# Two output stores moved to ScalarE's queue, transposing loads re-placed among stores, and three PSUM copies moved from VectorE to ScalarE

## The chip, the cores and the metric

One core of a Trainium2 chip runs the kernel. The metric is the device time of one execution in microseconds. The engines are named as in the profile: PE (TensorE), DVE (VectorE), ACT (ScalarE), POOL (GpSimd) and SP (SyncE, which here only issues DMAs). "SPq" and "ACTq" are instructions that these two spend on issuing DMAs.

## What is computed

The reference is a forward pass and its gradients. Shortened to what matters here:

```python
xn = layernorm(x)                                   # x: 2048 x 512
k_shift = sum over t of k[s + t - 3] * shift_k[:, 3 - t]
kv = k_shift * v
y = irfft(rfft(kv) * rfft(ssm_k)) + kv * ssm_D      # a convolution of length 2048
out = x + xn * y + ((xn @ w_gate) * (xn @ w_up)) @ w_down   # F = 1376
grads = vjp(out)(grad_out)    # for x, k, v, shift_k, ssm_k, ssm_D, w_gate, w_up, w_down
```

The outputs that the change touches are out_7 and out_8 (gradients of w_gate and w_up, 512 x 1376), out_9 (gradient of w_down, 1376 x 512), out_4 (gradient of shift_k, 512 x 4) and out_6 (gradient of ssm_D, 512). Out_0 to out_3 and out_5 (the result and the gradients of x, k, v and ssm_k) are only moved against them in SP's queue.

## The kernel before, in words

The kernel has two stages. In the first, up to about 304 us, it normalises x, runs the gated layer forward and back in eight chunks of 256 rows (`ffn1`, `yb`), and takes the convolution's signals through a two-step transform by matmuls, with DRAM in between (FD, GD). The hidden rows and their gradients (`hd`, three tensors of 1376 rows) go to DRAM as HDD.

The last stage is what the change is about. It interleaves four streams of work, all in one program order that the loop at the end of the kernel writes out:

- `dw()` goes over the eleven blocks of 128 hidden rows (`FBLK`, the last has 96). For each block it needs the hidden rows turned, so that the sequence lies on the partitions. For blocks 0 to 6 PE turns them (`hid_t`: load hb, 16 transposes, copy by ACT to nath or natd). For the last four (`TURNED`, blocks 7 to 10) a transposing DMA loads them as natT (`load_t`), except for the last chunk, which PE turns (`last_t`, copied by ACT to nat7). Then `down_grad` sums 16 matmuls into pd, which ACT copies to od, stored to out_9, and four times 16 matmuls go into pu, which ACT copies to og. Two blocks share one og, which two DMAs store to out_7 and out_8.
- `inv_y` and `inv_dk` (lines 944 and 989) take the inverse transforms: pq is copied by ACT to yC or dd, po to o5t. `put_dD` turns a column of o5t by PE (ptd), copies it to dDt and stores it to out_6.
- `dsk_gram` makes the gradient of shift_k: for four blocks of 128 columns, 32 matmuls into pk; DVE multiplies the result by the identity, reading PSUM, into kd, and sums it up (dsk). At the end dsk is turned by PE (pts), copied to dskt and stored to out_4.
- `ew` runs `final` and `bwd` for eight row blocks: DVE work with a load bb each and three stores (o, e, dk). What they have to store is kept in `late` and put out at the start of the next turn by `put_late`.

The tile framework orders instructions by priority and dependencies and sets every wait. A block under `tc.high_priority` goes ahead of its place in the program. `tc.issue_after(x)` puts the instructions traced in it behind x, if they are on x's engine. A tile's buffer is given out again when all that read or wrote its last tenant is done, a store of it included. Tiles with the same `tag` share their buffers: `tag="dd"` has two, used in turn by dd, kd, nat7, dskt and the last og. PSUM has three double banks (`P2`) and two single ones (`P1`). Each DMA also waits, on one of eight semaphores used in turn, until the DMA that had this semaphore before has landed. The queues of SP and ACT are worked off in order.

Before the change SP issues all of these loads and stores but two, and the transposing loads are placed by `behind` (line 800): block 9 after the newest bb load, block 10 after the newest og store, blocks 7 and 8 where priority puts them.

Of the kernel before, what the change touches and what calls it, by code (L numbers as in the profile page):

```python
# [9 lines left out]
F32 = mybir.dt.float32  # L10
I32 = mybir.dt.int32
ALU = mybir.AluOpType
ACTF = mybir.ActivationFunctionType
AX = mybir.AxisListType
# [7 lines left out]
P = 128  # L22
NC4 = 4
FBLK = [(i * 128, min(128, F - i * 128)) for i in range((F + 127) // 128)]
NFB = len(FBLK)
NCH = 8
SOON = 300
# [163 lines left out]
def kernel(  # L191
# [24 lines left out]
    nc = tc.nc  # L216
# [17 lines left out]
    def act(o, i):  # L234
        nc.scalar.copy(o, i)  # L235

    def dve(o, i):
        nc.vector.tensor_copy(o, i)  # L238
# [4 lines left out]
    BX = dram.tile([P, R, 2, D], BF, name="BX")  # L243
# [11 lines left out]
    def P1(name, shape, dt=F32):  # L255
        return ps1.tile(shape, dt, name=name, tag="p1")

    ident = const.tile([P, P], BF, name="ident")
# [397 lines left out]
    first = ExitStack()  # L656
# [131 lines left out]
    LG = {}  # L788
# [9 lines left out]
    TURNED = range(NFB - 4, NFB)  # L798

    def behind(fb):  # L800
        first = {NFB - 2: lambda: LG["bb"], NFB - 1: lambda: LG["og"]}.get(fb)
        return tc.issue_after(first().ins) if first else ExitStack()

    def load_t(fb):

        f0, fw = FBLK[fb]
        if fb == SPLIT:
            parts = ((0, 5, "n", dict(tag="natd", bufs=2)), (5, NCH - 1, "n", dict(tag="nath")))
        elif fw < P:
            parts = ((0, NCH - 1, "n", dict(tag="natd", bufs=2)),)  # L810
        else:
            parts = ((0, NCH - 1, "b", dict(tag="hb")),)
        nats[fb, 0] = {}
        for a, e, pool, kw in parts:
            t = CP[pool].tile([P, e - a, 3, 2, fw], BF, name="natT", **kw)
            with behind(fb) as _, tc.high_priority(offset=SOON):
                nc.sync.dma_start_transpose(out=t[:].rearrange("s c t h f -> s (c t h) f"),
                                            in_=HDD[:fw, fb, a:e].rearrange("p c t s -> p (c t s)"))
            for c in range(a, e):
                nats[fb, 0][c] = t[:, c - a]  # L820
# [13 lines left out]
    def nat_h(fb, r):  # L834
        f0, fw = FBLK[fb]
        if fb not in TURNED:
            return nats[fb, 0][:, r, :fw]
        return nats[fb, 0][r // 2][:, 0, r % 2, :] if r < R - 2 else nats[fb, 1][:, 0, r % 2, :fw]
# [7 lines left out]
    def hid_t(fb, t):  # L846
        if fb in TURNED:
            return
        f0, fw = FBLK[fb]
        hb = hbs.pop(fb) if t == 2 else hbs[fb]  # L850
        if t == 0:
            nats[fb, 0] = CP["n"].tile([P, R, P], BF, name="nath")
        elif t == 1:
            nats[fb, 1] = CP["n"].tile([P, 2, R, P], BF, name="natd", bufs=2)
        dst = nats[fb, 0] if t == 0 else nats[fb, 1][:, t - 1]
        pt = P2("pt", [P, R, P], BF)
        for r in range(R):
            hs = hb[:fw, r // 2, t] if r < R - 2 else hds[1][:fw, fb, t]
            nc.tensor.transpose(pt[:, r, :fw], hs[:, (r % 2) * 128:(r % 2) * 128 + 128], ident[:fw, :fw])  # L859
        act(dst[:, :, :fw], pt[:, :, :fw])  # L860
# [56 lines left out]
    c2b = ctx.enter_context(tc.tile_pool(name="c2b", bufs=2, side="right", reuse_waits="tile"))  # L917
# [8 lines left out]
    dsk = c2.tile([P, NC4, 4], F32, name="dsk")  # L926
# [86 lines left out]
    def put_dD(o5t):  # L1013
        act(dDs[:], o5t[:, :, 0, 0])
        yield
        pt = P1("ptd", [P, P], BF)
        nc.tensor.transpose(pt[:NC4, :], dDs[:], ident[:])
        dDt = c2.tile([NC4, P], BF, name="dDt")
        dve(dDt[:], pt[:NC4, :])
        nc.sync.dma_start(out_6.rearrange("(c p) -> c p", p=128), dDt[:])  # L1020

    def down_grad(fb):
        f0, fw = FBLK[fb]
        pd = P1("pd", [P, D])
        for r in range(R):
            nc.tensor.matmul(pd[:fw, :], lhsT=nat_h(fb, r), rhs=goC[:, r, :], start=(r == 0), stop=(r == R - 1))  # L1026
            if r == R // 2 - 1 and fb:
                hid_t(fb, 2)
                if fb + 2 < NFB:
                    load_h(fb + 2)  # L1030
        od = c2b.tile([P, D], BF, name="od")
        if fb + 1 < NFB:
            act(od[:fw], pd[:fw])
            nc.sync.dma_start(out_9[f0:f0 + fw, :], od[:fw])
        else:
            for h, cp, q in ((0, act, nc.scalar), (1, dve, nc.sync)):
                hc = slice(256 * h, 256 * h + 256)
                cp(od[:fw, hc], pd[:fw, hc])
                q.dma_start(out_9[f0:f0 + fw, hc], od[:fw, hc])

    def load_h(fb):
        (load_t if fb in TURNED else load_hb)(fb)

    def dw():
        og = None
        load_hb(2)
        for fb, (f0, fw) in enumerate(FBLK):
            last = fb + 1 == NFB
            if not last:
                down_grad(fb)  # L1050
                yield
                hid_t(fb + 1, 0)
                hid_t(fb + 1, 1)
                yield
                yield
            pu = P2("pu", [P, NC4, 2, P])
            if fb % 2 == 0:
                og = c2b.tile([P, 2, NC4, P], BF, name="og1", tag="dd") if last else c2.tile([P, 2, NC4, 2 * P], BF, name="og")
            q0 = (fb % 2) * P
            for c in range(NC4):  # L1060
                for r in range(R):
                    nc.tensor.matmul(pu[:, c, :, :fw], lhsT=xnC[:, r, cs(c)], rhs=nat_d(fb, r),  # L1062
                                     start=(r == 0), stop=(r == R - 1))
                if c == 1:
                    yield
                    if fb + 1 in TURNED:
                        last_t(fb + 1)
                    yield
            act(og[:, :, :, q0:q0 + fw].rearrange("p t c f -> p c t f"), pu[:, :, :, :fw])
            if fb % 2 == 1 or last:  # L1070
                a = f0 - q0
                for t, o in enumerate((out_7, out_8)):
                    LG["og"] = nc.sync.dma_start(o[:, a:f0 + fw].rearrange("(c p) f -> p c f", p=128), og[:, t, :, :q0 + fw])
            yield
            if last:
                down_grad(fb)
                yield

    def dsk_gram():
        for c in range(NC4):  # L1080
            pk = P2("pk", [P, 2, D])
            for r in range(R):
                for h in range(2):
                    c0 = c * 128 + 64 * h
                    nc.tensor.matmul(pk[64 * h:64 * h + 64, h, 0:256], lhsT=dks[:, r, c0:c0 + 64],
                                     rhs=KH[0][:, r:r + 4, c0:c0 + 64], start=(r == 0), stop=(r == R - 1))
            kd = c2b.tile([P, 4, 64], F32, name="kd", tag="dd")
            with tc.high_priority(offset=SOON):
                for h in range(2):
                    hs = slice(64 * h, 64 * h + 64)  # L1090
                    nc.vector.tensor_tensor(kd[hs], pk[hs, h, 0:256].rearrange("q (j c) -> q j c", j=4),
                                            ident[hs, hs].unsqueeze(1).to_broadcast((64, 4, 64)), op=ALU.mult)
                nc.vector.tensor_reduce(dsk[:, c, :], kd[:], axis=AX.X, op=ALU.add)
            yield
        dskb = c2.tile([P, 4, NC4], BF, name="dskb")
        nc.vector.tensor_copy(dskb[:], dsk[:].rearrange("q c i -> q i c"))
        for _ in range(2):
            yield
        pt = P1("pts", [P, 4, P], BF)
        for j in range(4):  # L1100
            nc.tensor.transpose(pt[:NC4, j, :], dskb[:, 3 - j, :], ident[:])
        dskt = c2b.tile([NC4, P, 4], BF, name="dskt", tag="dd")
        dve(dskt[:], pt[:NC4].rearrange("c j q -> c q j"))
        nc.sync.dma_start(out_4.rearrange("(c p) j -> c p j", p=128), dskt[:])
        yield

# [17 lines left out]

    def load_fin(b):
        bb = c2b.tile([P, 2, 2, D], BF, name="bb")
        LG["bb"] = nc.sync.dma_start(bb[:], BX[:, 2 * b:2 * b + 2, :, :])
        FL[b] = bb

    def final(b):  # L1130
# [47 lines left out]
    def put_late():  # L1178
        for dst, t in late:
            nc.sync.dma_start(dst, t[:])  # L1180
        late.clear()

    def ew():
        with tc.issue_after(DKS[2].ins):
            load_fin(0)
        yield
        for f in tail:
            put_late()
            f()
            yield  # L1190
        with tc.issue_after(LG["og"].ins):
            put_late()
        yield
# [45 lines left out]
```

## Time and profile before

| | |
|---|---|
| median of 3 runs | 480.83 us (479.9 to 481.28) |
| profiled execution | 481.82 us |
| its span, first to last instruction | 480.03 us |
| granted TensorE clock | 0.999 |
| PE busy in 304 to 384, 384 to 432, 432 to 476 us | 79.32 of 80, 46.46 of 48, 43.63 of 44 us |
| ACT busy in the same stretches | 50.20, 18.08, 13.70 us |
| DVE busy in the same stretches | 32.79, 41.92, 37.27 us |
| DMA, mean over the span | 291 GB/s, 139.85 MB |

How to read it: the busy time of an engine says little on its own. A stretch is set by the engine that hardly waits in it; what it still waits for is in the view of waits, which gives for each waiting instruction the one that released it, the total, the count and the longest. In the timelines a row merges instructions of one kind: start, duration, engine, line, operation, output and inputs, count, and in brackets the idle time before it with its releaser. The duration of a merged row of matmuls runs to the end of the last one; the next starts a little sooner, since matmuls are pipelined. Some matmul records are missing, so that a run of eight can show seven.

### The profile page before, as it was taken

To read this page: it belongs to the slowest core of one execution; us is meant where nothing else is said; L and a number is where in the kernel's file an instruction comes from. 1 tells how busy PE (TensorE), PEld (TensorE's weight loads), DVE (VectorE), ACT (ScalarE), POOL (GpSimd) and SP (SyncE) were. 2 spreads that over 40 slices of the span, in tenths; PEclk is the share of its full clock that TensorE was granted. 3 is DMA by queue.
4 is the path that set the end of the run, shared out by engine and by line. 5 is a ranking of instruction groups with operands and counts; after the bars stand their busy time and mean duration, and the time that the engine had idled before them with its cause. 6 is when DMAs were issued, how large, how long until landed. Compare 5 with 4: busy or idle time off the path is not lost.

```text
span 480.0 us, 10366 instructions
## 1 busy us (share of the span) xinstructions
PE 464.5 (97%) x4252; PEld 311.6 (65%) x4293; DVE 340.5 (71%) x609; ACT 305.6 (64%) x349; POOL 14.0 (3%) x30
## 2 busy tenths in 40 slices
PE   7999999999999999999999999999999999999996
PEld 6867755547648447447447743576777687677885
DVE  7889989979366567686777877022257899599893
ACT  4957677659568678779779975375576535233141
POOL 8000000000000000000000000110000000000000
PEclk9999999999999999999999999999999999999999
DMA  8999999989998968968978379999899979999858
GB/s 268 374 381 366 310 296 320 315 300 328 318 288 270 277 202 255 285 200 245 298 235 259 118 272 331 388 329 313 312 361 364 371 260 320 318 267 239 252 155 294
DMA packets 111132, 139.85 MB, mean 291 GB/s; under 512 B 38859, under 2 KB 84336, under 8 KB 109550
## 3 DMA queue, kind: packets, MB, share of 16 engines
q1 hardware_dynamic: 109502, 137.85, 89.7%
q10 hardware_dynamic: 1584, 1.36, 1.0%
q8 instruction: 33, 0.54, 0.5%
q14 instruction: 13, 0.11, 0.1%
HBM read 67.08 MB, written 63.41 MB: 272 GB/s over the span
## 4 chain that ended last, share of the span: by engine, by line
PE 67%; DMA 15%; DVE 14%; issue 2%; SPq 2%; ACT 1%; DVEq 0%; ACTq 0%
PE px L555 15%; PE pgu L512 13%; PE pu L1062 8%; PE py L548 7%; PE pdh L518 6%; PE pd L1026 4%; PE ps L584 3%; DMA khC<-in_A_k_dram 3%; PE pg L613 3%; DMA ssk<-in_A_ssm_k_dram 2%; PE pf L370 2%; PE pt L859 2%; DMA vb<-in_A_v_dram 2%; DMA kb<-KS 2%; DMA x_b<-in_A_q_dram 2%
## 5 line engine op out<-in xcount | busy, mean ns | idle before, releaser
L555 PE MATMUL px<-WT,hd 128*128 128x512 bf16 (+1 forms) x340 | 78.6, 379 | 1.6 <-issue 1.4
L1062 PEld LDWEIGHTS <-xnC 128*128 128x128 bf16 x704 | 67.0, 98 | 8.4 <-issue 0.6
L555 PEld LDWEIGHTS <-hd 128*128 128x128 bf16 (+1 forms) x352 | 32.8, 98 | 44.4 <-issue 7.7
L235 ACT CAST gu<-pgu 128x1024 bf16<-128x1024 f32 (+1 forms) x48 | 45.4, 946 | 16.9 <-PE pgu L512 16.7
L235 ACT CAST GO<-pg 128x1024 bf16<-128x1024 f32 x48 | 46.2, 1015 | 13.8 <-issue 7.2
L235 ACT CAST SP<-ps 128x1024 bf16<-128x1024 f32 x47 | 45.5, 1025 | 13.7 <-PE ps L584 11.8
L512 PE MATMUL pgu<-xt,Wu 128*128 128x256 bf16 (+1 forms) x352 | 53.1, 273 | 1.1 <-DVE kn L238 0.6
L600 DVE TENSOR_TENSOR T<-SP 128x2048 bf16<-128x2048 bf16 x24 | 29.3, 1222 | 34.8 <-ACT SP L235 34.7
L512 PE MATMUL pgu<-xt,Wg 128*128 128x256 bf16 (+1 forms) x352 | 52.8, 273 | 0.0
L1062 PE MATMUL pu<-natd,xnC 128*128 128x256 bf16 x448 | 51.2, 273 | 0.0
L518 PE MATMUL pdh<-gt,WdT 128*128 128x256 bf16 (+1 forms) x352 | 46.9, 273 | 0.1
L235 ACT CAST fst<-pf 128x1024 bf16<-128x1024 f32 x44 | 42.7, 1031 | 5.5 <-issue 2.3
L512 PEld LDWEIGHTS <-Wu 128*128 128x128 bf16 (+1 forms) x352 | 33.0, 100 | 15.6 <-issue 10.7
L548 PE MATMUL py<-Wd,hd 128*128 128x512 bf16 (+1 forms) x167 | 40.2, 379 | 0.8 <-issue 0.5
L235 ACT CAST og<-pu 128x1024 bf16<-128x1024 f32 (+1 forms) x11 | 10.9, 993 | 43.7 <-PE pu L1062 28.3
L518 PEld LDWEIGHTS <-WdT 128*128 128x128 bf16 (+1 forms) x352 | 34.9, 100 | 4.8
L512 PEld LDWEIGHTS <-Wg 128*128 128x128 bf16 (+1 forms) x352 | 34.8, 100 | 3.7
L235 ACT COPY natd<-pt 128x2048 bf16<-128x2048 bf16 x14 | 26.2, 1875 | 12.0 <-PE pt L859 12.0
L533 DVE TENSOR_TENSOR hd<-gu,dh 128x1024 bf16<-128x1024 bf16 (+1 forms) x48 | 30.8, 641 | 0.8
L532 DVE TENSOR_TENSOR hd<-gu 128x512 bf16<-128x512 bf16 (+1 forms) x48 | 19.0, 397 | 16.7 <-ACT gu L235 16.7
L548 PEld LDWEIGHTS <-hd 128*128 128x128 bf16 (+1 forms) x176 | 16.5, 98 | 20.8 <-issue 3.1
L600 DVE TENSOR_TENSOR U<-SP 128x2048 bf16<-128x2048 bf16 x24 | 29.2, 1218 | 0.0
(177 smaller groups left out, 687.4 us busy)
## 6 DMA issues: line engine op xcount, KB each, us to landing
HDD<-hd SPq DMA_DIRECT2D x35, 384.0 KB, 4.5
FD<-fst SPq DMA_DIRECT2D x24, 512.0 KB, 4.9
X<-FD SPq DMA_DIRECT2D x24, 512.0 KB, 5.5
GD<-GO SPq DMA_DIRECT2D x24, 512.0 KB, 3.9
g<-GD SPq DMA_DIRECT2D x11, 1024.0 KB, 8.9
hb<-HDD SPq DMA_DIRECT2D x7, 1344.0 KB, 10.2
bb<-BX SPq DMA_DIRECT2D x8, 512.0 KB, 5.5
BX<-bx SPq DMA_DIRECT2D x7, 512.0 KB, 3.9
```

Source lines behind the costliest of these rows:

```text
L235: nc.scalar.copy(o, i)
L512: nc.tensor.matmul(pgu[:w, i, t, :], lhsT=W[:, c, f0:f0 + w], rhs=xt[:, :, c, :], start=(c == 0), stop=(c == NC4 - 1))
L518: nc.tensor.matmul(pdh[:w, i, :], lhsT=WdT[:, c, f0:f0 + w], rhs=gt[:, :, c, :], start=(c == 0), stop=(c == NC4 - 1))
L532: nc.vector.tensor_tensor(hd[:fw, fb0:fb0 + n, 0, :], gu[:fw, :n, 0, :], gu[:fw, :n, 1, :], op=ALU.mult)
L533: nc.vector.tensor_tensor(hd[:fw, fb0:fb0 + n, 1:3, :], gu[:fw, :n], dh[:fw, :n].unsqueeze(2).to_broadcast((fw, n, 2, 256)), op=ALU.mult)
L548: nc.tensor.matmul(py[:], lhsT=hd[:fw, fb, 0, ss], rhs=Wd[:fw, fb, :], start=(fb == 0), stop=(fb == NFB - 1))
L555: nc.tensor.matmul(px[:], lhsT=hd[:fw, fb, t, ss], rhs=W[:fw, fb, :], start=(t == 1 and fb == 0), stop=(t == 2 and fb == NFB - 1))
L584: nc.tensor.matmul(ps[32 * q:32 * q + 32, a, :], lhsT=TB.EF[64 * a:64 * a + 64, 4 * g + q, ri].rearrange("p k j -> p (k j)"), rhs=X[64 * a ...
L600: tt(W[:].rearrange("p c a d -> p c (a d)"), A[:, i:i + 1].rearrange("p c a d -> p c (a d)").to_broadcast((P, 2, 2 * D)), B[:].rearrange(" ...
L613: nc.tensor.matmul(pg[q // 2][64 * a:64 * a + 64, q % 2, :], lhsT=TB.EI[32 * q:32 * q + 32, 2 * g + a, yi].rearrange("p k c -> p (k c)"), ...
L1026: nc.tensor.matmul(pd[:fw, :], lhsT=nat_h(fb, r), rhs=goC[:, r, :], start=(r == 0), stop=(r == R - 1))
L1062: nc.tensor.matmul(pu[:, c, :, :fw], lhsT=xnC[:, r, cs(c)], rhs=nat_d(fb, r), start=(r == 0), stop=(r == R - 1))
```

## The change

It does five things: the stores of od (all but the last block's) and of og are issued by ACT, behind the copies that make them; the transposing loads of blocks 9 and 10 are placed behind the newest bb load, and rounds of stores and later bb loads are placed behind the newest transposing load; the gram's sums are copied out of PSUM by ACT and multiplied in SBUF, without priority, with two blocks sharing one kd; dskt and dDt are copied by ACT instead of DVE; and the turning of dsk waits two turns longer.

```diff
     def behind(fb):
-        first = {NFB - 2: lambda: LG["bb"], NFB - 1: lambda: LG["og"]}.get(fb)
-        return tc.issue_after(first().ins) if first else ExitStack()
+        return tc.issue_after(LG["bb"].ins) if fb >= NFB - 2 else ExitStack()
...
-                nc.sync.dma_start_transpose(out=t[:].rearrange("s c t h f -> s (c t h) f"),
+                LG["t"] = nc.sync.dma_start_transpose(out=t[:].rearrange("s c t h f -> s (c t h) f"),
...
-        dve(dDt[:], pt[:NC4, :])
+        act(dDt[:], pt[:NC4, :])
...
             act(od[:fw], pd[:fw])
-            nc.sync.dma_start(out_9[f0:f0 + fw, :], od[:fw])
+            nc.scalar.dma_start(out_9[f0:f0 + fw, :], od[:fw])
...
-                    LG["og"] = nc.sync.dma_start(o[:, a:f0 + fw].rearrange("(c p) f -> p c f", p=128), og[:, t, :, :q0 + fw])
+                    LG["og"] = nc.scalar.dma_start(o[:, a:f0 + fw].rearrange("(c p) f -> p c f", p=128), og[:, t, :, :q0 + fw])
...
-            kd = c2b.tile([P, 4, 64], F32, name="kd", tag="dd")
-            with tc.high_priority(offset=SOON):
-                for h in range(2):
-                    hs = slice(64 * h, 64 * h + 64)
-                    nc.vector.tensor_tensor(kd[hs], pk[hs, h, 0:256].rearrange("q (j c) -> q j c", j=4),
-                                            ident[hs, hs].unsqueeze(1).to_broadcast((64, 4, 64)), op=ALU.mult)
-                nc.vector.tensor_reduce(dsk[:, c, :], kd[:], axis=AX.X, op=ALU.add)
+            if c % 2 == 0:
+                kd = c2b.tile([P, 2, 4, 64], F32, name="kd", tag="dd")
+            for h in range(2):
+                hs = slice(64 * h, 64 * h + 64)
+                act(kd[hs, c % 2], pk[hs, h, 0:256].rearrange("q (j c) -> q j c", j=4))
+                nc.vector.tensor_tensor(kd[hs, c % 2], kd[hs, c % 2], ident[hs, hs].unsqueeze(1).to_broadcast((64, 4, 64)), op=ALU.mult)
+            nc.vector.tensor_reduce(dsk[:, c, :], kd[:, c % 2], axis=AX.X, op=ALU.add)
             yield
...
-        for _ in range(2):
+        for _ in range(4):
             yield
...
-        dve(dskt[:], pt[:NC4].rearrange("c j q -> c q j"))
+        act(dskt[:], pt[:NC4].rearrange("c j q -> c q j"))
         nc.sync.dma_start(out_4.rearrange("(c p) j -> c p j", p=128), dskt[:])
...
         bb = c2b.tile([P, 2, 2, D], BF, name="bb")
-        LG["bb"] = nc.sync.dma_start(bb[:], BX[:, 2 * b:2 * b + 2, :, :])
+        with tc.issue_after(LG["t"].ins) if b > 4 else ExitStack():
+            LG["bb"] = nc.sync.dma_start(bb[:], BX[:, 2 * b:2 * b + 2, :, :])
...
         for f in tail:
-            put_late()
+            with tc.issue_after(LG["t"].ins) if "t" in LG else ExitStack():
+                put_late()
             f()
             yield
         with tc.issue_after(LG["og"].ins):
             put_late()
```

In SP's queue as built, 22 stores are gone. The first transposing load (block 7) now stands behind the o, e and dk stores and the bb load of that turn, which stood behind it. The second (block 8) stands ahead of the o and e stores of its turn. The pair for block 9 stands ahead of dskt's store, which stood ahead of it. The last (block 10) stands behind one bb load, with the o, e and dk stores after it. The dk store of the last `bwd` now stands ahead of the four o5t stores.

## The prediction

> **What bounds the kernel.** I read the page first, then PE's waits in the last stage, then PE's timeline around each wait, then SP's timeline and the chain of waits at the end.
>
> ```profile
> PE 464.5 (97%) x4252; PEld 311.6 (65%) x4293; DVE 340.5 (71%) x609; ACT 305.6 (64%) x349; POOL 14.0 (3%) x30
> PE   7999999999999999999999999999999999999996
> PEclk9999999999999999999999999999999999999999
> ```
>
> PE is busy in every slice at an undisturbed clock, and only the first slice and the last, where it ends early, are under 9. All edits lie behind 303.9 us, where the last stage begins, so the gain is what PE still waits for there. PE's and its weight loads' waits from 300 us on, with the total, the count and the longest:
>
> ```profile
> PE pt L859 <- DVE kd L1091: 1.3, 2, 1.1
> PEld L859 <- DVE kd L1091: 1.9, 2, 1.5
> PEld L859 <- DMA hb<-HDD: 0.7, 1, 0.7
> ```
>
> A third kind is counted as "issue". PE's timeline gives the sizes (start, duration, instructions):
>
> ```profile
> 413.80 1.06 PE L1001 MATMUL po<-IW,g 128*128 128x128 bf16 x16
> 414.91 1.67 PE L1026 MATMUL pd<-goC,nath 128*128 128x512 bf16 x7
> 417.64 0.95 PE L859 MATMUL pt<-ident,hb 128*128 128x128 bf16 x14 [1.06 <-DVE kd L1091]
> ...
> 428.91 3.19 PE L1026 MATMUL pd<-goC,natT 128*128 128x512 bf16 x13
> 431.93 0.59 PE L1026 MATMUL pd<-goC,nat 128*128 128x512 bf16 x2
> 432.63 0.22 PE L1017 MATMUL ptd<-ident,dDs 128*4 128x128 bf16 x1
> ```
>
> Undisturbed, 16 po take 0.90 (420.27 to 421.17) and eight pd take 1.73 (398.96 to 400.69). So pd began at 414.70 (one record of eight is missing) and was through at 416.43; pt began at 417.64: **1.2 us lost**, because the PSUM buffer that pt wants was still read by DVE for the gram (416.72 to 417.59), and DVE came late to it. In the same way pt at 401.96 should have come at 400.69+0.89 = 401.58 (0.38, and 0.11 in the 16 that follow): **0.49**. pt at 383.61 waits for the load of hb: 381.56+1.73 = 383.29, **0.3**. ptd at 432.63 should come at 428.91+3.46 = 432.37: **0.26**, the time until DVE has copied dskt (431.90 to 432.59). Sum: 2.25 us. The rest of the stage to 475.86 is packed, and then comes
>
> ```profile
> 472.39 3.47 PE pd L1026 x16
> 475.86 0.02 issue
> 475.88 0.38 ACT od L235
> 476.26 0.02 issue
> 476.28 0.42 DVE od L238
> ```
>
> with the last store behind it, unchanged by the edits: 480.03.
>
> **The change part by part.**
>
> *Gram's copies by ACT.* Removed: 8 products that DVE reads out of PSUM (0.42 each). Added: 8 copies 64x256 f32 on ACT; nearest row od 96x256 at 0.37, so 3.0 us. The products stay on DVE, reading SBUF, at 0.33 to 0.43 (the reduce and the present product); I keep 0.42. The pk buffers are now freed by ACT, which is not behind: pk of 402.96 and 408.43 end at 404.9 and 410.3, and ACT is idle from 405.5 to 414.0 in before. So the copies are done by 406.1 and 410.8; PE wants the buffers at 413 and 415.6. The copies of the first two pk (done 391.8 and 397.2) are wanted at 398 and 401.6. I take the whole **-1.69**. If ACT were late by more than 5 us at the last one, that gain would be gone.
>
> [...]
>
> *dskt and dDt by ACT, pts two turns later.* DVE gives up 0.68 and 0.20; ACT takes 0.2 to 0.8 each (dDs, nat), hidden in its gaps of 0.7 and 2.8. ptd now waits for ACT's od copy, with pts and half of po ahead of it: of the 0.26 I take **-0.2**.
>
> *22 stores by ACT* (10 od, 12 og). Cost on ACT: the only such rows are 0.35 and 0.36; on SP og took 0.5 to 1.1. I take 0.36 for od and 0.55 for og. Worst place: od, two yC copies, then pu, which wants the second yC's PSUM buffer: yC ends at 336.57, pu starts at 337.09. The store moves yC from 334.64 to about 334.83: 0.2 of a slack of 0.5, **nothing**. At 0.6 or more per issue PE would lose up to 0.3 in each of four rounds. An og pair follows og, where ACT idles 1.6 us (347.0 to 348.6): hidden. The stores also wait on ACT for an earlier DMA to land, since eight DMA semaphores go round among SP's and ACT's DMAs. Following each in the built program: od of 384.1 waits for a vb load (issued 378.3, landing 7.6) until about 385, holding nath back to 387; PE wants it at 389. og of 413 waits for the o and e stores behind the first transposing load (issue 408.8, landing 4.5), until about 414.5; natd behind it is wanted at 416.6. Nothing, with 1 to 2 us to spare.
>
> *SP without those stores.* SP no longer waits for ACT's od and og. bb goes out about 8 us sooner in the round of 345; khC, then the vb and kb behind it, 1.3 us sooner; hb of 368.24 about 1.5 sooner: **-0.3**. The skill ("DMA: Bandwidth & Descriptors", Issuing engines are not separate DMA queues) says that all queues share the same 16 engines and a second issuer saves only issue time. By that rule this 0.3 would stay away and the sum be 1.55 instead of 1.85; no run here shows it yet.
>
> *Transposing loads behind stores.* They hold SP for long:
>
> ```profile
> 399.05 9.69 SPq L817 DMA_TRANSPOSE natT<-HDD  x1
> ...
> 420.41 9.06 SPq L817 DMA_TRANSPOSE natT<-HDD  x1
> ...
> 432.61 0.29 SPq L1104 DMA_DIRECT2D out_dram<-dskt  x1
> ...
> 433.80 10.00 SPq L817 DMA_TRANSPOSE natT<-HDD  x2
> ```
>
> The first now follows the o, e, dk stores and the bb load that came at 408.79 to 410.36. DVE's waits of 4.29 (for o) and 1.09 (for bb) at 409 to 416 go, and with bb's earlier ones DVE ends about 6 us earlier, near 465.6 instead of 471.8. PE does not wait for that: nothing. The last transposing load moves from 452.94 to about 445; wanted at 466: nothing.
>
> But dskt's store went **ahead** of the pair of 433.80; now it stands behind it. And ACT's nat7 copy for block 8 takes dskt's buffer, so ACT, with og, od and o5t behind it, waits until that store has landed. The second load starts when PE has read hb, 416.4; 9.06 more; o, e, g, dk, bb 2.3; the pair 10.0; so dskt issues at about 437.8 and lands 2.9 to 3.7 later (dk, od): 441.1. nat7 (0.80) ends near 442; PE wants it, with all gains, at 444.92-2.25 = 442.7. Single transposing issues ran from 4.76 to 9.69, and the queue ahead of the pair (o, e, g, dk, bb: 2.25 MB at about 0.35 MB/us, 6.4 us) may hold its data back by 2 us: between 0 and 2 us lost. I take **+0.3**, near the rows as they stand, and **+0.05** for the small copies.
>
> Sum: -1.69-0.2-0.3+0.3+0.05 = -1.85. The profiled run took 481.82 (span 480.03, 1.79 around it), 0.99 above the median of the runs; the sum is set against the profile and taken off the median: 480.83-1.85 = **479.0**.
>
> **The rivals.**
>
> *Slower: ACT stuck behind dskt's store.* If the pair starts no earlier than before (433.8 to 443.8), the store lands at 446.8 to 447.6 and nat7 ends near 448; PE loses 5 us against 442.7, in all +2.8: 483.6 (482.3 to 484). It decides from a landing at 441.9, and from 444.1 the gain is gone. For it: SP's long rows, and the margin of under 1 us. Against it: SP reaches the second load without a wait, and that load hangs on PE itself. 0.13.
>
> *Same: the wait changes its engine.* Landings of 2 us more than the rows at og of 413 or at dskt cost PE 0.7 to 1.8 of the 1.85: 479.7 to 481. For: ACT is strictly in order, and three places have under 2 us to spare. 0.24.
>
> *The end is held by DMA.* SP's four o5t stores now stand behind the last dk. If DVE ended at 471.8 after all, 2.25 MB would start then instead of at 468.0; at the 0.40 MB/us of the window 474 to 476 that is 5.6 us, plus about 1.5 to start, and the last od behind it: about +1.5 at the end, 480.5. It decides from a DVE end of 469. 0.06.
>
> *It does not do what it says:* only the first and the last transposing load come behind stores; the second still holds back o, e, g and bb, and bb for the seventh round is wanted at about the time it lands (436). If DVE gains nothing, the forecast stands as long as the end does, since the gram's copies no longer hang on DVE.
>
> **How the numbers follow.** Forecast (478.4 to 479.6) 0.52, same 0.24, slower 0.13, end 0.06, and 0.05 for more gain than the counted gaps (477.6 to 478.4). The measurement tells about 0.3%, 1.44 us, so the border is 479.39, inside the forecast: of its 0.52 I put 0.46 below. Faster 0.51, within 0.3% 0.35, slower 0.14. The range 477.8 to 481.8 leaves out the slower rival and a little of the rest.
>
> **What would show it.** Right: no wait of PE for kd, ptd or hb; L817's second issue near 416 to 417; dskt's store landed before 442; DVE's last dk before 469; PE's end about 1.9 earlier and the tail of 4.2 us as before. Wrong: nat L235 waiting for a DMA on dskt, og or od copies released by DMAs, PE waiting for ACT at pd or pu after 410, or copies held up by the stores' issues.

## The result and the profile after

The changed kernel took 484.8 us (median of 6 runs, 483.02 to 487.07); the kernel before, timed beside it, 480.12 (6 runs, 478.96 to 481.28). The ratio is 1.010, 95% interval 1.0082 to 1.0119. It is slower, by about 4.7 us, and 5.8 us above the forecast. The changed kernel was run twice more beside the experiments: 1.0061 (1.0033 to 1.0089) and 1.0097 (1.0055 to 1.0138). The profiled execution took 484.0, its span is 482.2.

The page after, the same rows as were shown of before:

```profile
PE 466.9 (97%) x4252; PEld 313.3 (65%) x4293; DVE 339.1 (70%) x607; ACT 309.4 (64%) x359; POOL 13.9 (3%) x30
PE   8999999999999999999999999999999999997997
PEclk9999999999999999999999999999999999999899
```

PE has a slice of 7 in the 37th place, near 446 us, and the granted clock an 8 in the 38th, right behind it. Neither was there before. PE is also 2.4 us longer busy with the same 4252 instructions, most of it by the slower clock. Now PE's waits from 300 us on, and then ACT's longest:

```profile
PE pd L1025 <- ACT nat L235: 2.7, 1, 2.7
PE pt L858 <- DMA hb<-HDD: 0.5, 1, 0.5
```
```profile
ACT nat L235 <- DMA out_dram<-dskt: 12.0, 1, 12.0
```

The waits for kd, ptd's and the one for hb at 383.6 are gone, as forecast (the last not for the reason given, as the section on the prediction shows). In their place stands one wait for ACT's nat7 copy, and ACT waited 12 us for dskt's store. (The hb wait of 0.5 is of a load at 307 us, ahead of everything that was changed.) SP's timeline shows where that store stood, ACT's what hung on it:

```profile
399.42 11.94 SPq L816 DMA_TRANSPOSE natT<-HDD  x1
...
417.38 11.12 SPq L816 DMA_TRANSPOSE natT<-HDD  x1
...
431.83 10.79 SPq L816 DMA_TRANSPOSE natT<-HDD  x2
442.71 0.44 SPq L1103 DMA_DIRECT2D out_dram<-dskt  x1
```
```profile
431.37 0.57 ACT L235 COPY dskt<-pts 4x512 bf16<-4x512 bf16 x1
...
445.46 0.80 ACT L235 COPY nat<-pt 128x768 bf16<-128x768 bf16 x1 [11.99 <-DMA out_dram<-dskt]
```

dskt is ready at 431.94. Its store, 4 KB, is issued 10.8 us later, because the pair of transposing loads goes first and holds SP for 10.79 us. It lands at 445.4, and only then does ACT copy nat7. What PE made of it, in its timeline:

```profile
439.58 1.06 PE L1000 MATMUL po<-IW,g 128*128 128x128 bf16 x16
440.69 2.97 PE L1025 MATMUL pd<-goC,natT 128*128 128x512 bf16 x13
446.31 0.60 PE L1025 MATMUL pd<-goC,nat 128*128 128x512 bf16 x2 [2.66 <-ACT nat L235]
446.76 1.67 PE L1000 MATMUL po<-IW,g 128*128 128x128 bf16 x16
448.23 2.77 PE L1061 MATMUL pu<-natT,xnC 128*128 128x256 bf16 x14
...
475.28 3.19 PE L1025 MATMUL pd<-goC,natT 128*96 128x512 bf16 x14
```

The same places in the kernel before:

```profile
441.01 1.06 PE L1001 MATMUL po<-IW,g 128*128 128x128 bf16 x16
...
472.23 3.19 PE L1026 MATMUL pd<-goC,natT 128*96 128x512 bf16 x14
```

PE loses 2.66 us, and then more: the 16 po take 1.67 where such a row takes 1.06, the 14 pu 2.77 where they take 1.69. From 451.05 on the rows have their usual length. The view by stretches gives the granted clock, the number ahead of the last two:

```profile
444.00:452.00 8.00, 5.69 (x43) 4.63 (x44) 6.49 (x10) 4.23 (x5) 0.00 (x0) 0.79 1.10 266
```

It is 0.79, and 8 us at 0.21 less make **1.7 us** that no view of waits lists; in stretches of half a microsecond it is 0.50 for some 3.4 us, from 447.0 on. Up to 440 us PE was 1.43 us earlier than before; -1.43 + 2.66 + 1.7 is 2.9, and the last pd starts at 475.28 instead of 472.23, 3.05 later. The span is only 2.2 us longer: from the last od copy on ACT to the end it is 3.3 us here and was 4.15 in the profile of before.

### The profile page after: what moved, and what is told of

Its sections match the earlier page's. It is cut to its first block, busy times and chain, and to the rows that moved or that the text cites. A ratio compares the mean times of both kernels' runs of the same rounds, so it can differ in the third digit from the quotient of the medians.

```text
span 482.2 us, 10373 instructions
## 1 busy us (share of the span) xinstructions
PE 466.9 (97%) x4252; PEld 313.3 (65%) x4293; DVE 339.1 (70%) x607; ACT 309.4 (64%) x359; POOL 13.9 (3%) x30
## 4 chain that ended last, share of the span: by engine, by line
PE 80%; DMA 10%; DVE 5%; SPq 2%; issue 1%; ACT 1%; ACTq 0%
PE pu L1061 14%; PE px L555 14%; PE pgu L512 12%; PE pd L1025 7%; PE py L548 7%; PE pdh L518 6%; PE pt L858 4%; PE pq L931 3%; PE ps L584 3%; PE pg L613 3%; DMA ssk<-in_A_ssm_k_dram 3%; PE pf L370 2%; SPq L816 2%; DMA hb<-HDD 2%; DMA x_b<-in_A_q_dram 2%; PE pk L1084 2%
```

## The experiments

The theory: the loss is the place of dskt's store in SP's queue, through ACT's nat7 copy. The rivals: ACT's own store issues and waits, the stores of a second queue in flight, the gram's copies, the placement. Each kernel was timed beside the kernel before on its own chip; the ratio to that is given, since the chips differ a little (its median was 479.5 to 480.1).

**1. dskt's store by ACT** (from the changed kernel).

```diff
-        nc.sync.dma_start(out_4.rearrange("(c p) j -> c p j", p=128), dskt[:])
+        nc.scalar.dma_start(out_4.rearrange("(c p) j -> c p j", p=128), dskt[:])
```

> The changed kernel, but dskt's store is issued by ACT behind its copy instead of by SP behind the pair of transposing loads. Theory (the store's place): in the changed kernel ACT's nat7 copy waits 11.99 us for that store to land, PE loses 2.66 us to it and about 1.7 us to matmuls at a lower granted clock right behind; both go, and what the change gained before (1.43 us at block 8) and at the end (about 0.85 us) stays: 477.8 to 479. Rival (the 22 stores issued by ACT cost the time): ACT has one store more, so no better than the changed kernel, 484 to 485. Rival (two queues at once slow the transposing loads, and these hold PE): the loads stay as they are, 484.

Measured: 480.97, ratio 1.0037 (1.0008 to 1.0066). PE no longer waits for nat7, so most of the loss goes. But the expected gain over before does not appear. PE's timeline of the profiled execution (483.92) has two waits that the changed kernel's did not have, and ACT's shows the second one coming:

```profile
385.17 0.95 PE L858 MATMUL pt<-ident,hb 128*128 128x128 bf16 x14 [1.86 <-DMA hb<-HDD]
422.98 3.65 PE L1061 MATMUL pu<-natd,xnC 128*128 128x256 bf16 x32 [1.72 <-ACT natd L235]
```
```profile
418.12 1.91 ACTq L1072 DMA_DIRECT2D out_dram<-og  x2
420.15 1.01 ACT L235 CAST o5t<-po 128x1024 bf16<-128x1024 f32 x1 [3.97 <-DMA out_dram<-dk]
421.06 1.87 ACT L235 COPY natd<-pt 128x2048 bf16<-128x2048 bf16 x1
```

og is copied by 416.18, its pair of stores goes out only from 418.12 on. By the built program they wait, for their semaphores, on the o and e stores that SP issued at 414.12 and 414.79, landing 3.9 and 4.8 later (the brackets name dk, of the same queue); and those had stood behind the first transposing load, which here held SP from 400.60 for 13.47 us. o5t and natd stand behind og's stores on ACT.

**2. The kernel before, with dskt's store behind the pair**, and nothing else of the change.

```diff
+        if fb == SPLIT:                                   # in load_t, behind its loop
+            with tc.issue_after(LG["t"].ins), tc.high_priority(offset=SOON):
+                nc.sync.dma_start(out_4.rearrange("(c p) j -> c p j", p=128), LG["dskt"][:])
...
-        nc.sync.dma_start(out_4.rearrange("(c p) j -> c p j", p=128), dskt[:])
+        LG["dskt"] = dskt
```

> The kernel before, with one move: dskt's store stands behind the pair of transposing loads for block 9 in SP's queue instead of two DMAs ahead of it. No store by ACT, gram as before. Theory (the store's place): the pair of 433.8 to 443.8 goes first, the store lands at about 447, ACT's nat7 copy ends near 448 and PE, which wants it at 444.9, loses 3 us, and 1 to 2 us more if the clock falls behind such a wait: 483 to 485 against 480.1. Rivals (ACT's stores; the gram's copies on ACT): nothing of theirs is in this kernel, 480.

Measured: 481.34, ratio 1.0029 (1.001 to 1.0048): slower, by 1.5 us and not 3 to 5. The move costs by itself, with no store by ACT in the kernel. The size was off because SP, no longer waiting for dskt's copy, sent the pair at 430.66 instead of 433.8; the store went out at 440.45, and PE waited only 0.43 us for nat7 in the profiled execution (480.7), behind which the matmuls ran at their usual length. That is a third of the 1.5; what the rest is, the one profile does not show.

**3. The kernel before with the gram part alone**: the copies by ACT, four turns, and dskt's store by ACT so that it is behind no transposing load.

> The kernel before with the gram part alone: sums, dskt and dDt copied out of PSUM by ACT, four turns instead of two; dskt's store by ACT, so that it is behind no transposing load. Stores of od and og and all placements as before. Theory: PE's two waits for DVE's kd (1.3 us in the matmuls, 1.69 in starts) and the one for dskt's copy (0.2) go, 478.2 to 478.6. Rival (the copies on ACT cost as much as they free): 480 or more, with ACT waits ahead of pt at 401 and 415.

Measured: 479.18, ratio 0.9989 (0.9971 to 1.0007). The profiled execution (479.08) has no wait of PE from 300 us on, so the gram's copies cost nothing; the gain, about 0.6 us, is a third of the 1.69 forecast, and the interval holds 1.

**4. The changed kernel with two turns**: dskt is ready earlier, and its store then stands ahead of the pair.

```diff
-        for _ in range(4):
+        for _ in range(2):
             yield
         pt = P1("pts", [P, 4, P], BF)
```

> The changed kernel, but dsk is turned after two turns, as before the change, instead of four; in SP's queue as built dskt's store then stands ahead of the pair of transposing loads, with only dk and bb between. Theory (the store's place): nat7 waits for no DMA, PE for no nat7; 478 to 479.5 (pts may wait for DVE's dskb, as DVE is now off its old order: up to 0.5 us). Rival (ACT's stores, or the transposing loads themselves): 484.

Measured: 480.38, ratio 1.001 (0.9983 to 1.0037). SP's timeline:

```profile
428.57 0.45 SPq L1103 DMA_DIRECT2D out_dram<-dskt  x1
...
430.12 11.02 SPq L816 DMA_TRANSPOSE natT<-HDD  x2
```

The pair holds SP as long as in the changed kernel, but nothing hangs on what is behind it: neither nat7 nor PE waits. The profiled execution took 478.91, within 0.1 of the 479.0 that the prediction gave for the changed kernel, but the median misses the 478 to 479.5 expected here, and single executions took up to 484.96. One more was profiled:

> A second look at the changed kernel with two turns, for what its slower executions wait for: its first look was one of its fastest. Theory (hb of block 5): PE waits for hb at 383 us in proportion to the time over 478.9. Rival (late loads or ACT's stores): the wait stands behind 400 us. In both, no wait of PE for nat7 at block 8.

It took 480.25, 1.34 more than the one above. PE waited 0.86 us for hb at 384.56, and from the pt before to this one it took 3.64, 1.02 longer than the 2.62 above, without a wait. hb had gone out at 371.87, against 369.71 above and 368.24 in before. So at least this execution is explained by hb.

**5. The two kernels again, on one chip.**

> The changed kernel beside the next one on the same chip. Theory (the store's place): 482.5 to 484.8, 1.006 to 1.010 of the kernel before, with PE's wait for nat7 of 2 to 3 us in the profile, and 1.7 us more in the executions whose mean clock is 0.996. Rival (another part of the change): the next kernel is as slow.

> The changed kernel with two turns again: dskt's store ahead of the pair. Theory (the store's place): 2 to 3.5 us under the changed kernel on the same chip, 480 to 480.5, no wait of PE or ACT for dskt's store, what is left above the kernel before being PE's wait for hb at 383 us. Rival (another part of the change): within 1 us of the changed kernel.

Measured: 484.84 (ratio 1.0097, 1.0055 to 1.0138) and 481.78 (1.0048, 1.0021 to 1.0076). By the medians the store's place is worth 3.1 us here, though the two intervals overlap a little. The profile of the changed kernel (481.12) was of one of its quicker executions: the second transposing load took 9.69, PE waited 1.00 us for nat7, not the 2 to 3 expected, and the clock did not fall. The 480 to 480.5 expected of two turns was missed: on this chip it was 0.5% slower than the kernel before.

**6. Another execution of the changed kernel, profiled.**

> A second look at the changed kernel itself, for how the wait for nat7 varies between executions. Theory (the store's place): PE waits again 2 to 5 us at block 8's pd for nat7, and the matmuls behind it run at about half speed for some 3 us; the time over 482 is this wait. Rival: another wait, of hb or natd, has taken its place.

It took 481.77, and PE waited no less than in the first profile. But the matmuls behind the wait are not slow:

```profile
445.60 0.61 PE L1025 MATMUL pd<-goC,nat 128*128 128x512 bf16 x2 [2.82 <-ACT nat L235]
446.05 1.06 PE L1000 MATMUL po<-IW,g 128*128 128x128 bf16 x16
446.94 1.69 PE L1061 MATMUL pu<-natT,xnC 128*128 128x256 bf16 x14
```

The two executions differ by 2.2 us: 0.5 is hb at 307, 1.7 the clock. Over the three timings, 13 of 22 executions of the changed kernel had a mean clock under 0.998; with two turns 4 of 24, with the gram part alone none of 12, and of the kernel before 2 of some 140. The 13 have a median of 485.19, the nine others of 481.93. So a low clock goes with 3.3 us, twice what one such fall cost in the profile; and it is not all, since two of the nine took 484.01 and 485.11 at a full clock.

**7. PE's wait filled with work**: 12 matmuls of pd's shape into a PSUM bank of their own, ahead of the two that wait for nat7.

```diff
+            if fb == SPLIT - 1 and r == R - 2:
+                fill = P1("fill", [P, D])
+                for i in range(12):
+                    nc.tensor.matmul(fill[:], lhsT=nat_h(fb, i), rhs=goC[:, i, :], start=(i == 0), stop=(i == 11))
             nc.tensor.matmul(pd[:fw, :], lhsT=nat_h(fb, r), rhs=goC[:, r, :], start=(r == 0), stop=(r == R - 1))
```

> The changed kernel with 12 more matmuls of pd's shape (12 times 0.216 = 2.6 us) into a PSUM bank of their own, between block 8's last natT matmul and the two that wait for nat7; their sum is not used. All other orders are the same. Theory (PE lost 2.66 us to the wait and about 1.7 us more to the lower granted clock behind it): PE works through the wait, the clock stays at 1.0 and the 30 matmuls behind it take 0.9 and 1.69 us again; the end comes 1 to 2 us sooner than in the changed kernel, 483 to 484 against 484.8, although PE has more to do. Rival (the matmuls behind the wait were slow for another reason, say their operands): they stay slow, 484.8 or more.

Measured: 489.91, ratio 1.0202 (1.0171 to 1.0232), far slower, and so a miss as a time. In the profiled execution (490.56) the 16 po behind the filled wait took 1.06 and the 14 pu 1.69, as expected; but they took as little behind the unfilled wait of experiment 6, so this does not show that the filling did it. PE also waited 2.93 us for hb at 385.84. What was not foreseen is the next wait, on ACT and then on PE:

```profile
460.43 1.01 ACT L235 CAST o5t<-po 128x1024 bf16<-128x1024 f32 x1 [9.81 <-DMA natT<-HDD]
```
```profile
461.49 1.05 PE L1000 MATMUL po<-IW,g 128*128 128x128 bf16 x16 [4.22 <-ACT o5t L235]
462.66 4.59 PE L1029 MATMUL pd<-goC,natT 128*128 128x512 bf16 x13
```

In the program as built with the 12 matmuls, od's store, which ACT issued at 460.04, got the semaphore that the last transposing load had before; without them it had that of a bb load. So ACT stood for 9.4 us, from 450.61 on, until that load had landed, PE waited 4.22 for the PSUM buffer behind o5t, and the clock fell again (13 pd in 4.59 instead of 2.97).

**8. The 22 stores given back to SP**, gram and placement kept, dskt's store by ACT: from experiment 1,

```diff
-            nc.scalar.dma_start(out_9[f0:f0 + fw, :], od[:fw])
+            nc.sync.dma_start(out_9[f0:f0 + fw, :], od[:fw])
...
-                    LG["og"] = nc.scalar.dma_start(
+                    LG["og"] = nc.sync.dma_start(
```

> The changed kernel with dskt's store by ACT, and the stores of od and og given back to SP: gram by ACT and the new placement stay, ACT issues no od or og store. Theory (ACT's own stores cost the rest): ACT's stores waited for SP's DMAs (og of 418.1 for a dk store behind the first transposing load, og of 444.6 took 6.3 us), which made natd late by 1.7 us in the profiled run with the 22 stores by ACT; that goes, so 479.2 or less, the time of the gram part alone, and runs within 2 us of each other. Rival (the placement costs the rest): the loads and stores stand as in the changed kernel, 480.5 to 481 with runs up to 485.

Measured: 480.0, ratio 1.0004 (0.9988 to 1.002), no execution over 481.75, none with a low clock. Against a ratio of 1.0037 with the stores by ACT (experiment 1, on another chip, with an interval that overlaps) that points to ACT's stores; but it is not the 479.2 expected, and the profiled execution still waited 1.35 us for hb at 385.24.

**9. The 22 stores by POOL** (`nc.gpsimd` in the same two places), with two turns; all orders on PE, DVE and SP are those of experiment 4.

> The changed kernel with two turns (dskt's store ahead of the pair), and the 22 stores of od and og issued by POOL instead of ACT; the order of all instructions on PE, DVE and SP is the same as with the stores by ACT, only these rows leave ACT and stand on POOL, which has nothing else to do there. Theory (an ACT that waits in its stores makes natd, nath and o5t late): 478.4 to 479.2, no o5t or nath of ACT waits for a DMA because of a store ahead of it. Rival (two queues at once, or stores that start at a bad time, slow the loads hb, vb and the transposing loads): 480.4 or more, with runs up to 485, and the same waits for hb and vb. POOL's issues may be dearer than ACT's 0.35 us; nothing is behind them.

Measured: 481.01, ratio 1.0034 (1.0009 to 1.0059), up to 486.13, and 4 of 12 with a low clock. An ACT that is free of stores does not mend it. So ACT's own waiting is not the whole of what the second queue costs. The profiled execution (479.95) was not one of the slow ones, and what these wait for stays open.

**10. hb of block 5 sent early**, with two turns, and with the gram part alone.

```diff
-        nc.sync.dma_start(t[:fw], HDD[:fw, fb])
+        with tc.high_priority(offset=SOON) if fb == 5 else ExitStack():
+            nc.sync.dma_start(t[:fw], HDD[:fw, fb])
```

> The changed kernel with two turns, and one load more moved: hb of block 5 goes out behind the first khC load (at about 364.5) instead of behind khC, o, e and bb (369.7 in the profiled run with two turns). All else on PE and ACT as with two turns. Theory (what is left of the loss is PE's wait for hb at 383 us, because SP, waiting for a DMA's semaphore ahead of it, sends hb 1 to 3 us later than before the change): hb lands by 380, no PE wait at 383 us in any run, 479 to 479.6 and no run above 482. Rival (the rest is lost elsewhere, by ACT's stores among the late loads): 480.4 as with two turns, runs up to 485.

> The kernel before with the gram part alone (dskt's store by ACT), and hb of block 5 sent ahead of the khC loads (at about 363) instead of 366.6. Theory (hb's landing against PE's 383.3 costs the kernel before, too, 0.2 to 0.5 us in the profiled runs and none in the gram run): a little better than the gram part alone, 478.8 to 479.2, with the lowest runs as before, since hb already came in time in these. Rival (hb ahead pushes khC and vb back, and pk or inv_dk waits): 479.5 or more. This is the candidate to beat both kernels.

Measured: 479.54, ratio 0.9992 (0.9976 to 1.0008), and 479.0, ratio 0.9989 (0.9972 to 1.0006), the lowest median of all, though not clearly below the kernel before. With two turns the wait for hb is gone (pt at 383.13) and the median is 0.8 lower, within what the two intervals leave open. One execution, the profiled one (482.49), shows the remaining mechanism:

```profile
378.98 1.01 ACT L235 CAST og<-pu 128x1024 bf16<-128x1024 f32 x1 [2.43 <-PE pu L1062]
384.13 0.97 ACTq L1073 DMA_DIRECT2D out_dram<-og  x2
385.14 1.87 ACT L235 COPY natd<-pt 128x2048 bf16<-128x2048 bf16 x1 [5.15 <-PE pt L859]
```
```profile
387.06 5.32 PE L1062 MATMUL pu<-natd,xnC 128*128 128x256 bf16 x32 [1.98 <-ACT natd L235]
```

og's store waits from 379.99 to 384.13 for the DMAs that had the semaphores of the pair, by the built program a khC load and an o store that SP issued at 365.30 and 369.90, behind 2 MB of khC and the early hb. natd stands behind it, PE waits 1.98 us, and the 32 pu behind take 5.32 instead of 3.65. "PE pt" in the brackets names what natd itself needed, which had been there for 4 us: the engine named had long been done, and it was the store ahead.

**11. The changed kernel with hb early**, twice: the fourth corner of the two edits, the second time beside the changed kernel.

> The changed kernel as it is (four turns, dskt's store by SP behind the pair), with one load moved: hb of block 5 behind the first khC load, as in the kernel with two turns and hb early. It is the fourth corner of two edits, dskt's place and hb's place. Theory (the store's place is the large part, hb's place a small one beside it): the step from this kernel to two turns with hb early (479.5) is as large as from the changed kernel to two turns (4.4 us), so 483.5 to 484.5, with PE's wait for nat7 at block 8 of 2 to 4 us in the profile. Rival (a late hb makes the rest late, and the wait for nat7 with it): 480 to 481, the wait for nat7 under 1 us.

> The changed kernel with hb of block 5 early, again. Theory (the lengths belong to the kernel): 480.6 against 484 to 485.5 for the changed kernel on the same chip, the second load about 8 us, PE's wait for nat7 under 1 us. Rival (the execution): no nearer to the kernel before than the changed kernel, the second load longer than 9 us.

> The changed kernel again, beside the three below on one chip. Theory (the lengths belong to the kernel): 484 to 485.5, second transposing load 11 to 12 us on SP, PE's wait for nat7 2.5 to 5 us, and in most executions a mean clock of 0.996. Rival (they belong to the execution): 481 to 482 as in the second look, a second load anywhere between 7 and 12 us.

Measured: 480.64 (1.0024, 1.0002 to 1.0045); again 480.45 (1.0014, 0.9991 to 1.0038) beside 482.54 for the changed kernel (1.0061), which misses the 484 to 485.5 expected of it. The first expectation fell: the store still stands behind the pair, ACT still waits 10.1 us for it, and yet most of the loss is gone. The wait of PE for nat7 was 0.75 and 1.42 us, against 2.66, 2.82, 2.14 and 1.00 in four profiles of the changed kernel. It is not that PE came elsewhere, since it ran alike up to pt at 416.4 in both. The edit also reordered DVE's work, and with it a bb load and a dk store on SP, and the second transposing load, issued at 417.41 and 416.74, then held SP for 7.75 and 8.43 us, where it was 11.12, 11.52, 10.95 and 9.69 in those four. In the profile of the changed kernel taken here (482.94) the clock fell again, behind 2.14 us:

```profile
445.25 0.60 PE L1025 MATMUL pd<-goC,nat 128*128 128x512 bf16 x2 [2.14 <-ACT nat L235]
445.70 1.30 PE L1000 MATMUL po<-IW,g 128*128 128x128 bf16 x16
446.79 3.15 PE L1061 MATMUL pu<-natT,xnC 128*128 128x256 bf16 x14
```

**12. What sets that length**: the changed kernel without the og stores of blocks 4 and 5 (issued by ACT at 415.4), and without the o and e stores of row block 3 (issued by SP at 411.4), 512 KB each.

```diff
-                for t, o in enumerate((out_7, out_8)):
+                for t, o in enumerate((out_7, out_8) if fb != 5 else ()):
```
```diff
-        late.append((o0_n[:, rb, :], o))
+        if b != 3:
+            late.append((o0_n[:, rb, :], o))
...
-        late.append((o1_n[:, rb, :], e))
+        if b != 3:
+            late.append((o1_n[:, rb, :], e))
```

> The changed kernel without the two stores of og for blocks 4 and 5 (out_7 and out_8 are left unwritten there, 512 KB), which ACT issues at 415.4, 2 us ahead of the second transposing load. All other instructions are the same and in the same order. Theory (stores of another queue in flight hold a transposing load): the second load takes about 8 us instead of 11.1, dskt's store lands 3 us sooner, PE's wait for nat7 goes, 480 to 481. Rival (what is ahead counts by its bytes alone): 512 KB of some 3 MB less, at 0.3 MB/us 1.7 us less, 9.4 us, and PE still waits about 1 us: 482 to 483.

> The changed kernel without the o and e stores of row block 3 (out_0 and out_1 are left unwritten there, 512 KB), which SP issues at 411.4 and 412.1, between the first and the second transposing load. DVE's order shifts a little. Theory (another queue's stores hold a transposing load): og's stores stay in flight, the second load takes 10 to 11 us, 483 to 485. Rival (what is ahead counts by its bytes alone): as much as without the og stores, 9.4 us, 482 to 483.

Measured: 481.52 (1.0049, 1.0025 to 1.0073), second load 10.45, PE's wait 2.26; and 480.92 (1.0022, 1.0002 to 1.0042), second load 8.05, PE's wait 0.62. So the stores of the other queue hardly hold the load, and the theory put down for both falls; the same bytes ahead of it in SP's own queue seem to. But without o and e the load also started 1.9 us later (419.30), because hb was late in that execution, which left more time for what was ahead of it. How much of the 3 us is the bytes is not settled.

## Why the prediction was wrong

- **The step that failed is "+0.3", dskt's store behind the pair.** The chain was right (store, buffer, nat7, PE), its times were not. Forecast: second load at 416.4, 9.06, the five issues 2.3, the pair 10.0, landing 3.3 later, 441.1. Measured: 417.38 (SP waited until PE had read hb, not until it began to: 1.0), 11.12 (2.1 more), 3.3 (1.0 more), 10.88 (0.9 more), landing 2.65 later (0.65 less): 445.4, 4.3 late. In a chain of five DMA steps with a margin of under 1 us, each taken at its shortest or middle row, the margin was not there. Why the loads became longer stays open. The placement alone does not do it: with it, but with the stores on SP (experiment 8), the first two take 9.12 and 9.66, where they took 9.69 and 9.06 before. With the stores on ACT or POOL they run from 8.68 to 13.47 and from 6.69 to 11.52, and a load (hb) sent early, too, changes them (experiment 11).
- **The clock was not in the sum.** In the profiled execution the 2.66 us brought 1.7 more. The forecast counted a wait at its own length, and so did the slower rival: by its terms a landing at 445.4 is 1.3 past the 444.1 from which the gain is gone, and the time 480.83+1.3 = 482.1. The executions without a low clock have a median of 481.93, those with one 485.19; all six of the first timing had one.
- **The rival "ACT stuck behind dskt's store" came true**, with a chance of 0.13. Its condition (a landing later than 444.1) held; the reason given for it (a pair that starts no earlier than 433.8) did not, as the pair started at 431.83. Its 483.6 came from 5 us of waiting and no clock; the profile had 2.66 and 1.7, so that the figure lies near the measured 484.8 is in part luck.
- **"-1.69" for the gram was right in its mechanism**: the segment from pt at 401 to pt at 416 shrank from 15.68 to 14.45 us, the one ahead of it from 1.27 to 0.89, together 1.61. Its size was that of one execution. In another with the old gram (experiment 2) the two are 15.16 and 1.25, a gain of only 1.07, and in the timing it is 0.6. The profile of before was taken in an execution of 481.82, 2 us over the median of that kernel in most groups of runs (479.8). The forecast said that the sum is made against that execution, and then took all of it off the median. (Its terms as printed add up to -1.84, not -1.85, which changes nothing.)
- **"-0.2" for ptd** held: from pt at 416 to pu at 432 the stretch went from 16.05 to 15.86.
- **"-0.3" for SP without the stores** failed in its reason. hb went out at 370.89, 2.65 later than 368.24 and not 1.5 sooner, because an e store ahead of it on SP now waits 2.8 us for a g load that had its semaphore. That PE's wait for it is gone in the profile all the same is luck: the load landed 12.3 us after its issue and not 15.3, and PE came to it 0.7 us later. In the four profiles of the changed kernel PE does not wait for it at 383 us; in five of its versions (experiments 1, 4, 7, 8 and 12) it waits 0.86 to 2.93.
- **"Nothing" for the stores on ACT** holds for the issues (0.35 per od, 0.94 to 1.30 per pair of og; on SP a single og had taken 0.39 to 1.31, and not only 0.5 to 1.1) and for the copies of the gram (0.38 each). It does not hold for their waits: the place named in the forecast, og of 413 with natd behind it, cost PE 0.91 us in one profile of the changed kernel and 1.72 in experiment 1, and og of 380 with natd cost 1.98 in experiment 10.
- **DVE** ended at 467.6, 4.2 earlier (forecast 465.6), and it bought nothing, as forecast.
- **The end, taken as unchanged**, was 0.85 shorter (3.3 us from the last od copy on ACT, and not 4.15). It took 3.3 in experiment 2, too (475.64 to 478.9), with the old gram and stores, so this belongs to the execution of before that was profiled and not to the change.

So of the 2.7 to 5.1 us over the kernel before (three timings), the store's place makes some 3 to 4 by the medians (experiments 4 and 5), through the wait and the clock, and only as far as the loads ahead of it are long (experiment 11). What is left goes with the stores in a second queue (experiments 1, 8 and 9), of which the late hb and the held natd are seen in profiles, and their shares are not. That no version gets clearly below the kernel before is no contradiction: without any wait behind 383 us an execution takes 478.9, and the kernel before has a median of 479.8.

The Trainium skill ("DMA: Bandwidth & Descriptors", Issuing engines are not separate DMA queues) says that a second issuing engine saves only the time of the issue. By that the 0.3 would have stayed away, and hb indeed went out no sooner. The runs point further, since the kernels with a second issuer were the slower ones (experiments 1, 8 and 9).

## What to carry to other kernels

Before a store is moved behind a transposing load, look who takes its tile's buffer next: a 4 KB store that frees a buffer is on the path of the engine that wants the buffer, and all that is behind it on that engine. In this framework an engine that issues a DMA inherits the landing of another DMA, which a small edit elsewhere can exchange for a slower one; so a compute engine should issue stores only where it can stand idle for the longest transfer of the kernel. And sum gains against the same execution in which they were read: what is far above the median there is not there to be won in the others.

## What the runs showed of the hardware

- **A wait of PE can cost nearly twice its length.** Behind waits of 1.98 (experiment 10), 2.14 (the changed kernel in experiment 11), 2.66 (after) and 4.22 us (experiment 7) the granted clock was 0.50 for some 3.4 us, and the matmuls lost 1.67, 1.66, 1.7 and 1.62; behind 2.26 (without og, experiment 12), 2.82 (experiment 6) and 2.93 (hb, experiment 7) it did not fall. So the length alone does not decide. The Trainium skill ("TensorE: Matmul & The Clock Gate", HAM oscillation — how this bites in real kernels) warns of idle gaps of more than about 3.4 us; its 1.2 GHz for the array after such a gap, half the usual, and a free-running window of that length (What's actually happening) agree with the 1.7 lost and with the chance in it, but here gaps of 1.98 to 2.66 us were enough.
- **A transposing load of 42x128 elements per partition held its queue for 6.7 to 13.5 us** in these runs, and not for the 9 to 10 of one profile. What sets it is not settled (experiment 12).
- A 4 KB store issued by ACT while the pair of transposing loads was under way let the copy that hangs on it start at 442.91, 7.9 us after its issue at 435.04 (experiment 1), and 4.7 us after it in experiment 3; issued by SP behind the pair it was 2.75. So in another queue, too, such a store seems not to be free of the loads that are in flight.
